# Seven block products on fp16 for the keys and values of the second attention layer

## The chip, the cores and the metric

The kernel runs on one core of a Trainium2 chip. The core has a matrix engine (TensorE; PE in the profile, with its weight loads as PEld), three elementwise engines (VectorE, DVE; ScalarE, ACT; GpSimd, POOL), and SyncE, whose queue (SP, SPq) issues the DMAs. Each engine works through its own list of instructions in the order written; semaphores make one wait for another. Matrix products accumulate in PSUM, eight banks of 128 x 512 fp32; all else lies in SBUF. The metric is the device time of one launch in microseconds (us), lower is better, as the median of several runs.

## The reference

Four layers in a row, A, B, A, B, with the same two sets of weights both times. The input has 2048 rows of 1024 in bf16.

```python
def _A_ref(x, wqkv, wo):                 # 32 heads of 32
    qkv = (x @ wqkv).reshape(B, S, 3, H, Dh).transpose(2, 0, 3, 1, 4)
    phi = lambda t: jnp.where(t > 0, t + 1, jnp.exp(t)) + 1e-6
    pq, pk = phi(q), phi(k)
    kv = jnp.einsum("bhsd,bhse->bhde", pk, v)
    z = jnp.einsum("bhsd->bhd", pk)
    num = jnp.einsum("bhqd,bhde->bhqe", pq, kv)
    den = jnp.einsum("bhqd,bhd->bhq", pq, z)[..., None] + 1e-6
    return (num / den).transpose(0, 2, 1, 3).reshape(B, S, D) @ wo
def _B_ref(x, w_gate, w_up, w_down):     # F = 3584
    return ((x @ w_gate) * (x @ w_up)) @ w_down
x = x + _A_ref(layernorm(x), wqkv, wo)   # then B, then A, then B
```

## The kernel before

**Layout.** X, the running 2048 x 1024 input, stays in SBUF as 16 tiles of 128 rows. Working memory is dealt out by hand from three queues (class `Free`): 16 `slots` of 128 x 4096 bf16, 13 `temps` of 128 x 512 fp32, and the 8 PSUM `banks`; the one returned first is handed out first. A write into one of them waits for its last reader. No scheduler orders anything: each engine's order is the order of the program, with small plans (`at(step, ...)`) that hang other work behind a numbered step of matrix products. A step is mostly 4 or 8 matmuls of 128 x 128 by 128 x 512.

**Layer A (`layer_A`, li = 0 and 2).** First the keys and values: `kv_chunk` makes one 128 x 512 piece of K or V of one row tile, 8 matmuls (L386); there are 64 chunks, each in a bank of its own. A key piece goes through `phi` (Exp on ACT, L210; min and add, L211, and max and add, L212, on DVE) into `pks`; a value piece is copied by ACT (L396) into `vbs`. `kp` (L405) multiplies keys with values into three banks `kvp` that are held through the stage; the rows of one group of 512 are multiplied while the next group is computed. Layernorm of the later row tiles runs in the same stage: `ln_stats` (L172, L175, DVE), `ln_norm` (L181, L183 on ACT, then L185 on DVE), and `tr_tile`, a transposing DMA on SP (L197). After that come the queries (`q_step`, L508), the denominators (L522), and the output products (L538). `rows`, `scan` and `load_rows` of the first layer A also measure the norms of the B weights, from which `scale_begin` and `scale_end` (L283 to L296) make power-of-two scales, so that B can run on fp16.

**Layer B (`ffn_pass`, twice per layer; q = 0 to 3 over the kernel).** A pass handles 1024 rows. Its up stage (`quad`, j = 0 to 13, L667) already uses a seven-product form of a 2 x 2 block product: of 14 products of 4 matmuls per quad, which write 6 of the 8 banks, ACT copies partial sums out (L672, L678, L722), DVE adds and multiplies (L683, L686) into `hs`. Seven slots of `hs` hold h, each the h of two quads. For q = 0 and 1 the weights are cast to fp16 by ACT, four casts per quad (L329), and four sums of them are made by DVE (L344). Its down stage (`down_seven`, L889) runs seven products of 14 steps each, in the order 1, 5, 6, 3, 7, 2, 4, with 98 steps of 4 matmuls. Each product reads two pieces of `w_down` (7 steps each); after each piece `load_piece` (L619 from a cache in DRAM, L623 from the input) asks for the one three pieces later, and ACT casts the pieces of products 1, 3 and 2 (L634, two halves) 7 steps ahead of use. `s_sum` (L811) makes the sums of h; `after` (L862) reads the four banks of a finished product on DVE. Into the same steps the plan puts the layernorm of the next stage's row tiles: `ln_stats` at 2 + 7u, `ln_norm` at 4 + 7u, the transpose at 5 + 7u, for eight tiles u in the first pass and four in the second; in the second pass of the first layer B also the loads of the K and V weights of the second layer A (`load_a` at steps 16, 30, 44, 75).

SP's list matters twice. A transpose waits there for its normalised tile, and a load waits for its slot; everything behind it in the list waits too.

Of the kernel before, what the change touches and what calls it, by code (L numbers as in the profile page):

```python
# [10 lines left out]
ALU = mybir.AluOpType  # L11
# [8 lines left out]
HS = 2.0 ** -35  # L20

# [13 lines left out]
def kernel(  # L35
# [45 lines left out]
    slots = Free([const.tile([P, 4096], BF16, tag=f"s{i}", name=f"s{i}") for i in range(16)])  # L81
    temps = Free([const.tile([P, NB], F32, tag=f"f{i}", name=f"f{i}") for i in range(13)])
# [47 lines left out]
    mask = const.tile([P, P], F32, tag="mask", name="mask")  # L130
# [18 lines left out]
    wst = const.tile([P, 32, 6], F32, tag="wst", name="wst")  # L149
    dsq = const.tile([P, 8], F32, tag="dsq", name="dsq")  # L150
    dmx = const.tile([P, 6], F32, tag="dmx", name="dmx")
    bexp = const.tile([P, 3], F32, tag="bexp", name="bexp")
    scw = const.tile([P, 3], F32, tag="scw", name="scw")
# [8 lines left out]

    xnTs = {}
    xqs = {}
    lns = {}
# [10 lines left out]

    def ln_norm(li, t):
# [6 lines left out]
        xn = xnp.tile([P, D], F16 if half else BF16, tag="xn", name="xn")  # L184
# [4 lines left out]
    def tr_tile(li, t):  # L189
# [5 lines left out]
        xnT = (h3 if li % 2 == 1 else v3)(s, NB)  # L195
# [11 lines left out]
    def phi(b, dst):  # L207
        m = temps.get()
        e = m[:].bitcast(BF16)[:, 0:NB]
        nc.scalar.activation(out=e, in_=b[:], func=ACT.Exp)  # L210
        nc.vector.tensor_scalar(out=e, in0=e, scalar1=1.0, scalar2=1e-6, op0=ALU.min, op1=ALU.add)  # L211
        nc.vector.scalar_tensor_tensor(out=dst, in0=b[:], scalar=0.0, in1=e, op0=ALU.max, op1=ALU.add)  # L212
        temps.put(m)
# [14 lines left out]

    def load_rows(r):
# [14 lines left out]
    qsum = {}  # L244

    def norm_sums(m, q):
        if m == 0:
# [3 lines left out]
            nc.vector.bn_aggr(out=mv[:], in_=wst[:])  # L251
# [3 lines left out]
                                           op0=ALU.mult, op1=ALU.add)  # L255
        else:
# [5 lines left out]
    def scale_begin(m):  # L262
        n = 2 - m
        q = small.tile([P, 2], F32, tag="wq2", name="wq2", bufs=1)
# [4 lines left out]
        qb = t[:].bitcast(BF16)[:, 0:2 * P].rearrange("p (m n) -> p m n", n=P)  # L269
# [5 lines left out]
    def scale_end(m):  # L275
        n = 2 - m
        q, t, qb = qsum.pop(m)
        b = banks.get()
        pt = b[:].bitcast(BF16)[:, 0:2 * P].rearrange("p (m n) -> p m n", n=P)
# [5 lines left out]
        e = bexp[:, 2 * m:2 * m + n]  # L285
# [5 lines left out]
        sc = scw[:, 2 * m:2 * m + n]  # L291
        nc.vector.reciprocal(out=sc, in_=e)
        nc.vector.tensor_scalar(out=sc, in0=sc, scalar1=WS, scalar2=None, op0=ALU.mult)
# [82 lines left out]
    def layer_A(li, ahead):  # L376
        pks = {}
        kvp = [banks.get() for _ in range(3)]
# [80 lines left out]

        kvx = slots.get()  # L460
# [88 lines left out]
        for i in range(NQ + OLAG):  # L549
# [4 lines left out]
            if i == 0:  # L554
                for t in range(NT - TPG, NT):
                    kp(t)
# [427 lines left out]
```

## Time and profile before

| what | us |
|---|---|
| three runs | 1510.39, 1510.46, 1511.22 (median 1510.46) |
| the profiled execution | 1511.85, of which the span on the core is 1509.8 |
| first layer A, to the first matmul of layer B | 251.56 |
| first layer B: up, down, up, down | 169.22, 84.61, 169.21, 84.61 |
| keys and values of the second layer A | 116.17 (759.21 to 875.38) |
| rest of the second layer A | 123.36 (875.38 to 998.74) |
| second layer B: up, down, up, down | 169.21, 84.61, 169.21, 84.62 |

The stage times are read from the timeline of TensorE and from the chain of work that ended last. The page names a group of instructions as line, engine, operation, output <- input by the program's names, shape, count, then busy time, mean duration in ns, and the engine's idle time just before with what ended it. A matmul's mean of 379 ns is its whole passage; matmuls overlap, and what counts is the distance between starts. The granted clock of TensorE is 1.00 in every stage.

### The profile page before, as it was taken

The page shows a single profiled execution, that of the slowest core. Times are in us where ns is not written, and L with a number is a line of the kernel's source. Part 1 is how long each engine was busy: PE and PEld are TensorE (multiplying, and loading weights), DVE is VectorE, ACT ScalarE, POOL GpSimd, SP SyncE. Part 2 cuts the span into 40 slices and gives each one's busy share as a digit, 9 for nine tenths or more (in the row PEclk, how much of TensorE's full clock was granted, in tenths as well). Part 3 has the DMA queues.
Part 4 walks back from the last instruction along what each step waited for, and adds up shares of the span by engine and source line. Part 5 has one row for each costly group of instructions (what it writes and reads, how often), then busy time and mean ns, then how long its engine had stood idle before and what let it go on. Part 6 is the DMA issues. An engine that isn't in the chain of part 4 may idle for free.

```text
span 1509.8 us, 18303 instructions
## 1 busy us (share of the span) xinstructions
PE 1500.2 (99%) x7122; PEld 689.6 (46%) x7170; DVE 940.1 (62%) x1596; ACT 737.0 (49%) x1115; POOL 90.3 (6%) x46
## 2 busy tenths in 40 slices
PE   9999999999999999999999999999999999999999
PEld 4454444444444444444445444444444444444444
DVE  6567989988686666667255466864444853444452
ACT  4678875767534577662133365533335223333420
POOL 0000004972000000000000000000000000000000
PEclk9999999999999999999999999999999999999999
DMA  8696246464348788749413300563333678333523
GB/s 244 165 305 206 84 91 193 147 208 143 130 126 252 240 263 254 259 174 256 151 29 84 84 1 5 149 237 140 140 115 126 170 252 348 112 140 140 195 74 129
DMA packets 213415, 247.61 MB, mean 164 GB/s; under 512 B 68432, under 2 KB 189264, under 8 KB 202576
## 3 DMA queue, kind: packets, MB, share of 16 engines
q1 hardware_dynamic: 213328, 246.44, 51.9%
q8 instruction: 56, 0.92, 0.3%
q14 instruction: 31, 0.25, 0.1%
HBM read 189.79 MB, written 40.89 MB: 153 GB/s over the span
## 4 chain that ended last, share of the span: by engine, by line
PE 98%; DVE 1%; DMA 1%; issue 0%; SPq 0%; DVEq 0%
PE b L667 45%; PE b L889 22%; PE b L386 14%; PE b L508 7%; PE b L538 7%; PE b L405 1%; PE b L522 1%; DMA s<-in_A_wqkv_dram 1%; PE b L490 0%; DVE st L172 0%; DVE X L540 0%; SPq L92 0%; DVE s L530 0%; DVE xn L185 0%; SPq L98 0%
## 5 line engine op out<-in xcount | busy, mean ns | idle before, releaser
L667 PE MATMUL b<-s,s 128*128 128x512 f16 x3136 | 677.5, 379 | 0.0
L667 PEld LDWEIGHTS <-s 128*128 128x128 f16 x3136 | 306.8, 98 | 370.0
L889 PE MATMUL b<-s,s 128*128 128x512 f16 x1568 | 339.1, 379 | 0.0
L683 DVE TENSOR_TENSOR f<-f,b 128x512 f32<-128x512 f32 x232 | 159.1, 687 | 226.9 <-ACT f L672 212.4
L672 ACT COPY f<-b 128x512 f32<-128x512 f32 x284 | 166.0, 584 | 224.8 <-PE b L667 224.8
L889 PEld LDWEIGHTS <-s 128*128 128x128 f16 x1568 | 153.4, 98 | 185.0
L386 PE MATMUL b<-s,s 128*128 128x512 bf16 x1000 | 221.5, 379 | 3.1 <-DMA s<-in_A_wqkv_dram 1.6
L386 PEld LDWEIGHTS <-s 128*128 128x128 bf16 x1024 | 99.7, 98 | 121.3 <-issue 2.2
L634 ACT ACTIVATE s<-s,scw 128x1792 f16<-128x1792 bf16 x48 | 83.1, 1785 | 90.8 <-DMA s<-in_B_w_down_dram 54.4
L210 ACT ACTIVATE f<-b 128x512 bf16<-128x512 f32 x128 | 75.6, 596 | 105.9 <-PE b L386 83.5
L329 ACT ACTIVATE s<-s,scw 128x1024 f16<-128x1024 bf16 x112 | 123.0, 1151 | 3.8 <-DMA s<-in_B_w_gate_dram 3.5
L678 ACT COPY b<-b 128x512 f32<-128x512 f32 x104 | 59.2, 570 | 128.3 <-PE b L667 128.3
L508 PE MATMUL b<-s,s 128*128 128x512 bf16 x504 | 119.5, 379 | 0.3
L538 PE MATMUL b<-s,s 128*128 128x512 bf16 x496 | 117.7, 379 | 1.1 <-DVE s L530 0.3
L592 POOL TENSOR_SCALAR s<-s,scw 128x1024 f16<-128x1024 bf16 x28 | 88.6, 3182 | 258.9 <-DVE X L540 245.0
L686 DVE SCALAR_TENSOR_TENSOR s<-f,b 128x512 f16<-128x512 f32 x108 | 74.2, 687 | 40.1 <-PE b L667 24.4
L211 DVE TENSOR_SCALAR f<-f 128x512 bf16<-128x512 bf16 x128 | 36.9, 288 | 81.0 <-ACT f L210 80.4
L686 DVE SCALAR_TENSOR_TENSOR s<-f,f 128x512 f16<-128x512 f32 x116 | 83.2, 718 | 4.0
L172 DVE BATCH_NORM_STATS2 st<-X 128x6 f32<-128x512 bf16 x128 | 81.9, 680 | 3.5 <-DMA X<-in_A_x_dram 3.5
L538 PEld LDWEIGHTS <-s 128*128 128x128 bf16 x512 | 50.0, 98 | 61.0 <-DVE s L530 1.0
L508 PEld LDWEIGHTS <-s 128*128 128x128 bf16 x512 | 50.0, 98 | 59.6
L862 DVE SCALAR_TENSOR_TENSOR X<-b,kap,f 128x512 bf16<-128x512 f32 x48 | 32.7, 743 | 60.6 <-PE b L889 60.6
(84 smaller groups left out, 859.1 us busy)
## 6 DMA issues: line engine op xcount, KB each, us to landing
s<-wc SPq DMA_DIRECT2D x56, 1024.0 KB, 6.6
s<-dc SPq DMA_DIRECT2D x32, 896.0 KB, 5.9
wc<-s SPq DMA_DIRECT2D x28, 1024.0 KB, 4.8
s<-in_B_w_down_dram SPq DMA_DIRECT2D x24, 896.0 KB, 5.2
s<-in_B_w_down_dram SPq DMA_DIRECT2D x14, 1024.0 KB, 7.4
s<-in_B_w_gate_dram SPq DMA_DIRECT2D x28, 512.0 KB, 5.7
s<-in_B_w_up_dram SPq DMA_DIRECT2D x28, 512.0 KB, 6.4
s<-in_A_wqkv_dram SPq DMA_DIRECT2D x11, 1024.0 KB, 9.7
```

What stands on the lines that cost most here:

```text
L172: nc.vector.bn_stats(out=st[:, c, :], in_=X[:, t, c * FMAX:(c + 1) * FMAX])
L329: nc.scalar.activation(out=h, in_=v, func=ACT.Copy, scale=scw[:, m:m + 1])
L386: nc.tensor.matmul(out=b[:], lhsT=xnT[:, k, tl * P:(tl + 1) * P], rhs=w[:, k, :], start=(k == 0), stop=(k == KD - 1))
L508: nc.tensor.matmul(out=b[:], lhsT=w[:, k, j * P:(j + 1) * P], rhs=xnT[:, k, :], start=(k == 0), stop=(k == KD - 1))
L538: nc.tensor.matmul(out=b[:], lhsT=v3(pqs[g], G)[:, c, tl * P:(tl + 1) * P], rhs=v3(M[n], NB)[:, c, :], start=(c == 0), stop=(c == KD - 1))
L592: nc.gpsimd.tensor_scalar(out=h3(s, D)[:, i, :], in0=v3(s, D)[:, i, :], scalar1=scw[:, 2:3], scalar2=None, op0=ALU.mult)
L634: nc.scalar.activation(out=v.bitcast(F16)[:, r * w:(r + 1) * w], in_=v[:, r * w:(r + 1) * w], func=ACT.Copy, scale=scw[:, 2:3])
L667: nc.tensor.matmul(out=o[m][:], lhsT=W.get(j, m, st[i - 1], k), rhs=mv[i - 1][:, k, :], start=start and k == 0, stop=stop and k == KH - 1, ...
L672: nc.scalar.copy(out=d[m][:], in_=o[m][:])
L683: nc.vector.tensor_tensor(out=d[m][:], in0=d[m][:], in1=o[m][:], op=ALU.add)
L686: nc.vector.scalar_tensor_tensor(out=hv[:, 2 * (j % 2) + r, g * G:(g + 1) * G], in0=x[:], scalar=HS, in1=y[:], op0=ALU.mult, op1=ALU.mult)
L889: nc.tensor.matmul(out=bank[(key, tl)][:], lhsT=lhs(i, j, tl), rhs=h3(wd[2 * pi + j // WPC], NB)[:, j % WPC, :], start=(j == 0 and i in (1 ...
```

## The change

In the second layer A (li = 2) keys and values are no longer made by `kv_chunk` but by a new `kv_seven`, the same seven-product scheme as in layer B. The code of `kv_chunk` stays, as `kv_eight`, for the first layer A. A unit u (0 to 7) handles four blocks: two row tiles and two more of the same 512-row group (`tiles(u)`), against two column halves of K and of V. It runs 14 products of 4 matmuls (names like `6k`: product 6 for the keys), in five banks, which with `kvp` are all eight. A bank takes several products one after the other, with copies by ACT in between.

For this the weights and the normalised rows of that layer are fp16. The norms of K, Q and V weights are measured in the first down stage (`scan_a`: six loads of 1 MB, twelve squares on ACT), the scales made around quads 0 and 1 of the second pass (`scale_begin(2)`, `scale_end(2)`). The second down stage gets 16 casts of K and V weights on ACT (`cast_a`), their sums (`w_sum`), the layernorm of eight row tiles instead of four, and the first group's row sums (`x_sum`) on DVE. The other eight row tiles are normalised inside `kv_seven`, where ACT applies the norm (`ln_apply`) instead of DVE, and where the query weights are loaded and cast as well. Query, denominator and `kvm` take the scales along as operands. The products of keys and values that are left for the first query step (`rest`) are those of the last unit: 2 tiles instead of 4.

`hs` is cut otherwise: one slot holds the h of quads 0 and 1, and from quad 2 on, four quads share two slots, one for each column half `a`; the slots of half 0 are free after the sums of product 7, not only in product 4. There are 17 slots and 12 temps, one of which holds the statistics `wst` until the first scales are made in the first layer A; the block mask is bf16.

```diff
-    slots = Free([const.tile([P, 4096], BF16, tag=f"s{i}", name=f"s{i}") for i in range(16)])
-    temps = Free([const.tile([P, NB], F32, tag=f"f{i}", name=f"f{i}") for i in range(13)])
+    slots = Free([const.tile([P, 4096], BF16, tag=f"s{i}", name=f"s{i}") for i in range(17)])
+    temps = Free([const.tile([P, NB], F32, tag=f"f{i}", name=f"f{i}") for i in range(12)])
...
-    mask = const.tile([P, P], F32, tag="mask", name="mask")
+    mask = const.tile([P, P], BF16, tag="mask", name="mask")
...
-    wst = const.tile([P, 32, 6], F32, tag="wst", name="wst")
+    wtmp = temps.get()
+    wst = wtmp[:][:, 0:192].rearrange("p (c s) -> p c s", s=6)
...
+    ACOL = (1, 0, 2)
...
+    def cast_a(m, n, i):
+        s = wA["kqv"[m]][n]
+        nc.scalar.activation(out=h3(s, NB)[:, 2 * i:2 * i + 2, :], in_=v3(s, NB)[:, 2 * i:2 * i + 2, :],
+                             func=ACT.Copy, scale=scw[:, 3 + m:4 + m])
...
+    def w_sum(which, i):
+        if which not in wS:
+            wS[which] = slots.get()
+            if "d" not in wS:
+                wS["d"] = slots.get()
+        a11, a12, a21, a22, c, d = w_blocks(which)
+        s1, s2 = c[:, 0:KH], c[:, KH:KD]
+        o, x, y, op = ((s1, a21, a22, ALU.add), (s2, s1, a11, ALU.subtract), (d, a11, a21, ALU.subtract),
+                       (a21, a12, s2, ALU.subtract))[i]
+        nc.vector.tensor_tensor(out=o, in0=x, in1=y, op=op)
...
+        t1, t2, t3, t4 = (t[:, j] for j in range(4))
+        o, x, y = ((t1, b12, b11), (t2, b22, t1), (t3, b22, b12), (t4, b21, t2))[i]
+        nc.vector.tensor_tensor(out=o, in0=x, in1=y, op=ALU.subtract)
...
+    def ln_rstd(li, t):
+        mv = lns[(li, t)]
+        rstd = small.tile([P, 1], F32, tag="rstd", name="rstd")
+        nc.scalar.activation(out=rstd[:], in_=mv[:, 1:2], func=ACT.Ln, bias=eps5[:], scale=1.0)
+        nc.scalar.activation(out=rstd[:], in_=rstd[:], func=ACT.Exp, scale=-0.5)
+        nmr = small.tile([P, 1], F32, tag="nmr", name="nmr")
+        nc.vector.tensor_scalar(out=nmr[:], in0=mv[:, 0:1], scalar1=rstd[:], scalar2=-1.0, op0=ALU.mult, op1=ALU.mult)
+        lns[(li, t)] = rstd, nmr
+
+    def ln_apply(li, t):
+        rstd, nmr = lns[(li, t)]
+        xn = xnp.tile([P, D], F16, tag="xn", name="xn")
+        nc.scalar.activation(out=xn[:], in_=X[:, t, :], func=ACT.Identity, bias=nmr[:], scale=rstd[:])
+        lns[(li, t)] = xn
...
+            nc.scalar.activation(out=e, in_=b[:], func=ACT.Exp, bias=lns2[:, c:c + 1], scale=kaps[:, c:c + 1])
+            nc.vector.tensor_scalar(out=e, in0=e, scalar1=scw[:, 3 + c:4 + c], scalar2=epss[:, c:c + 1],
+                                    op0=ALU.min, op1=ALU.add)
...
+    def scan_a(i, h, got={}):
+        if h < 0:
+            got[i] = load_cols(wqkv_v, ACOL[i // 2] * DC + i % 2)
+            return
+        s = got[i]
+        v = s[:, 2048 * h:2048 * h + 2048]
+        c = i % 2 * 2 + h
+        nc.scalar.activation(out=v, in_=v, func=ACT.Square, accum_out=asq[:, i // 2, c:c + 1])
+        if h == 1:
+            slots.put(s)
...
+        elif m == 2:
+            nc.vector.tensor_reduce(out=q[:, 0:3], in_=asq[:], axis=AX.X, op=ALU.add)
+            nc.vector.tensor_scalar(out=q[:, 0:2], in0=q[:, 0:2], scalar1=2.0 ** -27, scalar2=None, op0=ALU.max)
...
+        nc.vector.tensor_scalar(out=sc, in0=sc, scalar1=AS if m == 2 else WS, scalar2=None, op0=ALU.mult)
+        if m == 2:
+            nc.vector.tensor_scalar(out=kaps[:], in0=e, scalar1=1.0 / AS, scalar2=None, op0=ALU.mult)
+            nc.scalar.activation(out=lns2[:], in_=sc[:, 0:2], func=ACT.Ln)
+            nc.vector.tensor_scalar(out=epss[:, 0:2], in0=sc[:, 0:2], scalar1=1e-6, scalar2=None, op0=ALU.mult)
+            nc.vector.tensor_tensor(out=epss[:, 2:3], in0=epss[:, 0:1], in1=sc[:, 1:2], op=ALU.mult)
...
+    def kv_seven(kvp):
+        plan = {}
+
+        def at(step, f, *args):
+            plan.setdefault(step, []).append((f, args))
+
+        for t in range(2 * TPG, NT):
+            i = 4 + 9 * (t - 2 * TPG)
+            at(i, ln_stats, 2, t, (0,))
+            at(i + 1, ln_stats, 2, t, (1,))
+            at(i + 3, ln_rstd, 2, t)
+            at(i + 5, ln_apply, 2, t)
+            at(i + 6, tr_tile, 2, t)
+        for g, i in ((1, 15), (2, 46), (3, 76)):
+            for j in range(4):
+                at(i + 2 * j, x_sum, g, j)
+        at(20, load_w, "q", 0)
+        at(21, load_w, "q", 1)
+        for n in range(DC):
+            for i in range(4):
+                at(31 + 11 * n + 2 * i, cast_a, 1, n, i)
+        at(92, lambda: wA.update(o=[load_cols(wo_v, n) for n in range(DC)]))
+
...
+        SEQ = "1k 5k 1v 6k 2k 6v 7k 5v 7v 2v 4k 3k 4v 3v"
...
+            for j, step in enumerate(SEQ.split()):
+                i, w = int(step[0]), step[1]
+                key = "b" if i == 2 else ("c" if i in (3, 5) else "a") + w
+                if key not in bk:
+                    bk[key] = banks.get()
+                if i == 1 and w == "k":
+                    bk["b"] = banks.get()
+                b = bk[key]
+                rhs = w_rhs(w, i)
+                for k in range(KH):
+                    nc.tensor.matmul(out=b[:], lhsT=lhs[i][:, k, pr * P:(pr + 1) * P], rhs=rhs[:, k, :],
+                                     start=k == 0 and (i in (1, 5) or i == 2 and w == "v"), stop=k == KH - 1,
+                                     skip_group_check=True)
+                if i == 1:
+                    if w == "k":
+                        nc.scalar.copy(out=bk["b"][:], in_=b[:])
+                    else:
+                        copy("1v", b)
+                elif i == 6:
+                    copy("6" + w, b)
+                elif i == 7:
+                    copy("7" + w, b)
+                    if w == "k":
+                        add(tm["7k"][:], "7k", bk["ck"])
+                        phi(tm["7k"], pk(1, 1), 0)
+                    else:
+                        add(vb(1, 1), "7v", bk["cv"])
+                    temps.put(tm.pop("7" + w))
+                elif i == 3:
+                    if w == "k":
+                        add(tm["6k"][:], "6k", b)
+                        phi(tm["6k"], pk(1, 0), 0)
+                    else:
+                        add(vb(1, 0), "6v", b)
+                    temps.put(tm.pop("6" + w))
+                    banks.put(bk.pop(key))
+                elif i == 2:
+                    if w == "k":
+                        phi(b, pk(0, 0), 0)
+                    else:
+                        add(vb(0, 0), "1v", b)
+                        temps.put(tm.pop("1v"))
+                        banks.put(bk.pop("b"))
+                elif i == 4:
+                    if w == "k":
+                        phi(b, pk(0, 1), 0)
+                    else:
+                        nc.scalar.copy(out=vb(0, 1), in_=w4(b))
+                    banks.put(bk.pop(key))
+                for f, args in plan.get(u * 14 + j, ()):
+                    f(*args)
+
...
+        for u in range(2 * NG):
+            unit(u)
+            if u > 0:
+                for t in tiles(u - 1):
+                    kp(t, u == 1 and t == 0, False)
+            if u % 2 == 1:
+                slots.put(xgs.pop(u // 2))
...
+        rest = kv_eight(li, kvp) if li == 0 else kv_seven(kvp)
...
+                        nc.vector.scalar_tensor_tensor(out=kvm[:, 3 * b + j, :], in0=src[:, j, 0:P],
+                                                       scalar=kaps[:, 2:3], in1=mask[:], op0=ALU.mult, op1=ALU.mult)
...
-                for t in range(NT - TPG, NT):
-                    kp(t)
+                rest()
...
+    def hpos(a, j):
+        return (0, 2 * a + j) if j < 2 else (1 + 2 * ((j - 2) // 4) + a, (j - 2) % 4)
...
-            if j % 2 == 0:
+            if j == 0:
                 hs.append(slots.get())
-            hv = h3(hs[j // 2], 2 * G)
+            elif j % 4 == 2:
+                hs.extend([slots.get(), slots.get()])
...
+            if q == 1 and j == 0:
+                scale_begin(2)
+            if q == 1 and j == 1:
+                scale_end(2)
...
+            if i == 7 and r in (2, 4, 6):
+                slots.put(hs[r - 1])
...
-            for u in range(2 * TPG if p == 0 else TPG):
+            for u in range(2 * TPG):
                 t = nl[1] * 2 * TPG + u
-                at(2 + 7 * u, ln_stats, nl[0], t)
-                at(4 + 7 * u, ln_norm, nl[0], t)
-                at(5 + 7 * u, tr_tile, nl[0], t)
+                i = 2 + 7 * u if p == 0 or u < TPG else 56 + 9 * (u - TPG)
+                at(i, ln_stats, nl[0], t)
+                at(i + 2, ln_norm, nl[0], t)
+                at(i + 3, tr_tile, nl[0], t)
...
+                    for i in range(6):
+                        at(2 + 9 * i, scan_a, i, -1)
+                        at(10 + 9 * i, scan_a, i, 0)
+                        at(13 + 9 * i, scan_a, i, 1)
...
-                at(16, load_a, "k", 0)
-                at(30, load_a, "k", 1)
-                at(44, load_a, "v", 0)
-                at(75, load_a, "v", 1)
+                for i, (t0, t1, m) in enumerate(((10, 20, 0), (24, 34, 0), (38, 48, 2), (58, 68, 2))):
+                    at(t0, load_w, "kqv"[m], i % 2)
+                    for j in range(4):
+                        at(t1 + 2 * j, cast_a, m, i % 2, j)
+                for j in range(4):
+                    at(64 + 2 * j, w_sum, "k", j)
+                    at(79 + 2 * j, w_sum, "v", j)
+                    at(72 + 2 * j, x_sum, 0, j)
```

(`w_blocks`, `w_rhs` and `x_blocks`, left out, only name parts of the slots; `copy` and `add` inside a unit are an ACT copy from a bank to a temp and a DVE add of a temp and a bank.)

## Prediction

> **What bounds the kernel now.** I read first the page's busy times and the chain that ended last, then the stages one by one as windows, then the timelines of ACT and DVE at the places that the change touches.
>
> ```profile
> PE 1500.2 (99%) x7122; PEld 689.6 (46%) x7170; DVE 940.1 (62%) x1596; ACT 737.0 (49%) x1115; POOL 90.3 (6%) x46
> ...
> PE 98%; DVE 1%; DMA 1%; issue 0%; SPq 0%; DVEq 0%
> ...
> 251.73 169.22 PE b L667 x784
> ```
>
> TensorE is never without work, so time is the number of matmuls. 784 of them take 169.22 us, 0.2158 each; 4 (a step) take 0.863. The windows (busy time of PE, PEld, DVE, ACT, POOL; clock; DMA) show how much room the others have where the change puts work:
>
> ```profile
> 420.78:505.39 84.61, 84.61 (x393) 38.35 (x392) 60.42 (x100) 29.79 (x34) 0.00 (x0) 1.00 0.70 213
> ...
> 674.60:759.21 84.61, 84.61 (x394) 38.34 (x392) 43.72 (x72) 19.16 (x18) 0.00 (x0) 1.00 0.61 182
> 759.21:875.38 116.17, 115.54 (x598) 55.77 (x609) 56.37 (x116) 42.02 (x87) 0.00 (x0) 1.00 0.27 64
> ```
>
> First and second down stage, and the keys and values (KV): half-empty ACT and DVE. The prices come from these rows (groups, then timelines of ACT and DVE):
>
> ```profile
> L212 DVE SCALAR_TENSOR_TENSOR s<-b,f 128x512 bf16<-128x512 f32 x32 | 22.1, 692 | 1.1
> L210 ACT ACTIVATE f<-b 128x512 bf16<-128x512 f32 x32 | 19.1, 597 | 62.8 <-PE b L386 61.7 <-remote 1.1
> ...
> 506.45 0.58 ACT L672 COPY f<-b 128x512 f32<-128x512 f32 x1 [11.31 <-PE b L667]
> ...
> 514.71 3.23 ACT L329 ACTIVATE s<-s,scw 128x1024 f16<-128x1024 bf16 x3
> 518.60 0.57 ACT L678 COPY b<-b 128x512 f32<-128x512 f32 x1 [0.67 <-PE b L667]
> ...
> 521.40 0.68 DVE L344 TENSOR_TENSOR s<-s,s 128x1024 f16<-128x1024 f16 x1
> ...
> 178.87 0.42 DVE L283 TENSOR_REDUCE wq<-b 128x2 f32<-128x256 bf16 x1
> 179.32 0.17 DVE L287 TENSOR_SCALAR bexp<-wq 128x2 int32<-128x2 int32 x1
> ```
>
> A copy starts 0.2 after its product's last step (506.45 against 505.39 + 0.863). ACT starts back to back 0.1 early (copy or Exp 0.5, cast 1.07), DVE 0.08 early (0.61 per add, `bn_stats` or 128x1024 fp16 sum). ACT to DVE takes 0.04; I take 0.05 towards PE.
>
> **The change, part by part.**
>
> *Removed.* 64 chunks x 8 = 512 matmuls become 8 units x 14 x 4 = 448: -64 x 0.2158 = -13.8 us, all on the path. fp16 costs what bf16 costs (379 ns in both groups of the page). `kp` is the same 16 tiles.
>
> *The KV stage's two other queues.* A unit is 14 x 0.863 + 0.945 for two tiles of `kp` = 13.03 us. ACT has 7 copies and 4 Exps (5.5 us), DVE 5 adds and 4 phi pairs (about 7). Walked through in order, such a unit has no PE wait: the tightest copies (of 1, 6 and 6v, whose bank takes the next product two steps = 1.73 later) have 1.73 - 0.2 - 0.58 - 0.05 = 0.9 to spare. But extras stand in the same lists, in front of these copies: per layernorm tile 2 `bn_stats`, an aggregate (0.21) and a small product on DVE, 0.5 of rstd and 1.15 of `ln_apply` (by L329, same size) on ACT; in units 1, 3 and 5 four `x_sum` of 0.69 on DVE; in units 2 and 3 eight casts of 1.15 on ACT. One such extra eats the 0.9, two do not fit. And ACT stands still where an Exp waits for DVE's add (product 7 or 3), or rstd for DVE's aggregate. Five of eight banks in rotation, all in use, leave PE nothing else to do.
>
> I walked units 0 to 5 by these prices, PE, ACT and DVE lists side by side, time from the stage's start. The boundary of units 1 and 2 as an example: in unit 1 DVE has 24 instructions, 12.6 us, from 14.2 on; the last, the key add of product 3, ends at 28.0, and product 5 of unit 2, wanted at 27.33, overwrites its bank: 0.72. Behind that add ACT runs Exp to 28.64, rstd to 29.07, copy 4v to 29.55: 1v, wanted at 28.91, waits 0.69. Then `ln_apply` 29.9 to 31.05, and only then the copy of 1k to 31.5: 6k, wanted at 30.46, waits 1.11. Sums: entering unit 1 0.8, in it 0.5, entering unit 2 2.5, in it 0.8, entering unit 3 1.0, in it (four casts, a norm, three x_sums) 3.5, entering unit 4 2.6, in 5 0.5, in 0, 6 and 7 nothing. Together +12.2. Bounds: 0 (the stage before shows no such wait, though with a fresh bank per chunk; nothing here can gain beyond the matmuls), and 20 (some 80 ACT instructions in the loaded units without their 0.1 overlap: +8). I take the walk, since its rows are of the same instructions.
>
> *Scales at quads 0 and 1 of the second pass.* Three transposes: +0.2 (L281: two in 0.28). `scale_end(2)` ends in a Ln on ACT that waits for a DVE chain, and stands ahead of quad 1's first copies; product 6 of that quad waits for the first copy. DVE is busy with four weight sums until 522.0. Then the reduce (0.42 for 256 columns, 0.28 for 128: 0.56 for 384), five dependent small ones at 0.2, done at 523.6; Ln (0.29, by rstd's 294 ns) to 523.9; the copy, 518.60 before, to 524.5. Product 6 was due at 505.39 + 12.08 + 0.2 + 2.59 = 520.3. PE waits +4.2. Bounds 3.5 and 5: order and durations are all shown; only handovers are open. Behind the Ln stand no loads; DVE and ACT are level again in quad 1.
> [...] In this trace the granted clock is 1.00 throughout and no PE gap exceeds 1.5 us, so no row shows what a 4 us gap does. [...]
>
> *First down stage: `scan_a`.* Twelve squares of 128x2048 (L237: 1.90 + 0.19) are 25 us more on ACT, beside 30 of 84.6; six loads of 1 MB go into a DMA share of 0.70. ACT's list is in order: a square that waits for its load holds up rstd of the next tile, so DVE's xn, so that tile's transpose on SP, so the `w_down` piece behind it. Landings come from the second down stage:
>
> ```profile
> s<-in_A_wqkv_dram SPq DMA_DIRECT2D x1, 1024.0 KB, 9.7
> ...
> s<-in_B_w_down_dram SPq DMA_DIRECT2D x1, 896.0 KB, 9.8
> ```
>
> That is, 9.7 behind another piece, 9.8 for a piece behind such a load, against 5.5 alone. So scan 2, issued at 440.2 behind piece 5, lands at 449.9, its squares end at 453.8, transpose 4 goes from 451.7 to 454.9, piece 7 lands at 462, and its cast, also behind scan 3, has its first half at 463.6, wanted at 463.1: 0.5. Transpose 6 moves from 463.8 to 466.6, piece 9 stands behind scan 5 and lands at 476 to 478, wanted at 475.7. I take +1.5; bounds 0 (pieces land in 5.5) and 4 (each of pieces 7 and 9 at 9.8 behind a late transpose).
>
> *Second down stage.* ACT +16 casts (18 us on 19), DVE four tiles, eight `w_sum` (1.22 by L368), four `x_sum`: 66 of 84.6. Piece 6's cast stands behind one cast_a, piece 7's behind three; each still ends about 1 us before its use. DVE is behind from step 56 on but done by step 93 of 98; SP's four more transposes stand ahead of piece 11, which leaves at step 63 as it did before (729.6). POOL's list is unchanged. So 0; bounds 0 and 2 (both covers gone).
>
> *No cost taken.* 12 temps: a temp returns after some 7 us, DVE's lag is under 1. `hs`, `rest`, scaled phi, `kvm`, bf16 mask: same sizes and counts per stage; loads of weights still wait for slots freed 10 to 13 steps before the cast. Cover gone: under 1 us each.
>
> **Sum.** -13.8 + 12.2 + 0.2 + 4.2 + 1.5 = +4.3. Against the profiled execution (1511.85: span 1509.8 and 2.05 around it) 1516.2; that execution lies 1.4 above the median of the runs, 1510.46, so **1514.8** is forecast.
>
> **Rivals.** *The queues keep up (faster).* Place: the copies of products 1 and 6 in units 1 to 4. For it: by busy time ACT has some 24 us of work in 26 of units 2 and 3, which fits if waits do not add up. Price: no KV wait at all gives 1510.46 - 13.8 + 0.2 + 4.2 + 0 = 1501.1; with half of the walk's waits and the scan's 1.5, 1508.7. It decides when KV and scan waits together stay under 6.4. Against it: 0.9 of slack against casts of 1.07.
> *A wash.* These waits between 6.4 and 12.4: 1507.4 to 1513.5.
> *The first down stage becomes bound by its pieces.* Each late piece delays rstd, transposes and the next piece; SP's order speaks for it, and that TensorE's own delay gives it back against it. With 4 instead of 1.5, and 3 more in KV: 1520.
> *The stage does not shorten at all* would need slower fp16 matmuls: excluded by the 379 ns of both.
>
> **How the numbers follow.** A measurement tells 0.2% (3 us) from nothing. Chances: forecast and worse, 1513.5 to 1518, 0.42; over 1518, 0.16; the wash 0.24; under 1507.4 0.18. Slower 0.58, same 0.24, faster 0.18. Range: 1506 (5 of the 12 us of KV waits, none at the scans) to 1520, which leaves out about two in ten; the forecast's own range is 1511 to 1518.
>
> **What would show it.** In the new profile: 448 fp16 matmuls in a KV stage of about 115 us; PE waits there for ACT copies and DVE adds, most in units 1 to 3, none in the last two; one gap of 4 us three products into quad 1 of the second pass, released by ACT; waits under 2 us in the first down stage, released by ACT's cast or a DMA. Wrong if the KV stage is under 108 us (lists keep up), if the gap at quad 1 is missing, or if waits appear in stages that I priced at nothing, the second down stage above all.

## The result and the profile after

The changed kernel takes 1520.88 us (median of 6 runs, 1519.95 to 1521.35) against 1510.61 for the kernel before, run beside it: ratio 1.0066, 95% interval 1.0053 to 1.0079. It is slower, as forecast, but by 10.3 us instead of 4.3, and 0.9 us past the upper end of the range. The profiled execution took 1521.27 us, with a span of 1519.5; that of before had 1509.8, so 9.7 us have to be found.

The page of the changed kernel (busy times, then the chain that ended last, by engine):

```profile
PE 1495.6 (98%) x7109; PEld 683.2 (45%) x7109; DVE 987.5 (65%) x1675; ACT 814.7 (54%) x1196; POOL 89.6 (6%) x46
...
PE 92%; DVE 4%; ACT 3%; DMA 1%; issue 0%; SPq 0%; DVEq 0%
```

TensorE is busy for less time than before (1495.6 instead of 1500.2), and yet the span is longer: the chain now runs through DVE and ACT for 7% of it. The five largest waits of TensorE in the whole kernel say where (line waiting, releaser, us in total, times, longest):

```profile
PE b L539 <- ACT f L523: 5.1, 7, 1.4
PE b L539 <- DVE f L526: 4.6, 5, 1.3
PE b L909 <- ACT b L920: 4.0, 1, 4.0
PE b L539 <- ACT vb L576: 1.9, 5, 0.7
PE b L539 <- ACT b L544: 1.7, 2, 1.1
```

L539 is the product of the KV stage, L909 that of the up stages. The windows of the first down stage, the second, the KV stage, and the second up stage (PE, PEld, DVE, ACT, POOL; granted clock; DMA):

```profile
419.70:504.31 84.61, 84.61 (x394) 38.31 (x393) 60.15 (x100) 52.18 (x58) 0.00 (x0) 1.00 0.93 288
680.37:764.98 84.61, 84.61 (x394) 38.31 (x392) 62.70 (x100) 37.46 (x42) 0.00 (x0) 1.00 0.66 194
764.98:886.03 121.05, 107.23 (x561) 50.29 (x560) 79.45 (x149) 73.85 (x119) 0.00 (x0) 1.00 0.21 53
504.31:680.37 176.06, 172.10 (x788) 77.42 (x787) 111.57 (x179) 115.51 (x163) 0.00 (x0) 0.98 0.73 233
```

Both down stages are as long as before to the hundredth. The KV stage is 121.05. Its window holds 14 tiles of `kp`, where the window of before (116.17) holds 12, so like against like it is 121.05 against 117.1: +3.9. Without any wait it would be 448 x 0.2158 + 14 x 0.4725 = 103.3, so the waits cost 17.7. The waits listed for L539 add up to less, 13.8 with a small sixth one, because a profile counts an idle time from the modelled end of a matmul, 379 ns after its start, while the next could have started after 216: each of the twenty waits costs some 0.16 more than it shows, 3.3 together. The second up stage took 176.06 instead of 169.22: +6.84. Its one gap, on PE, ACT and DVE, in three timelines:

```profile
516.56 2.75 PE L909 MATMUL b<-s,s 128*128 128x512 f16 x12
523.27 2.29 PE L909 MATMUL b<-s,s 128*128 128x512 f16 x5 [3.96 <-ACT b L920]
```

```profile
522.53 0.20 ACT L381 ACTIVATE lns<-scw 128x2 f32<-128x2 f32 x1 [5.69 <-DVE scw L378]
522.64 1.06 ACT L920 COPY b<-b 128x512 f32<-128x512 f32 x2
```

```profile
520.32 0.69 DVE L434 TENSOR_TENSOR s<-s,s 128x1024 f16<-128x1024 f16 x1
520.92 0.55 DVE L368 TENSOR_REDUCE wq<-b 128x3 f32<-128x384 bf16 x1
521.51 0.17 DVE L372 TENSOR_SCALAR bexp<-wq 128x3 int32<-128x3 int32 x1
```

The copies of the quad stand behind the Ln, the Ln behind the chain of DVE, the chain behind four weight sums: 3.96 us, 4.2 forecast. From the gap on the window view (TensorE alone; the third number from the end is the granted clock) has

```profile
520.00:522.00 2.00, 0.00 (x0) 0.92 0.20 82
522.00:523.00 1.00, 0.00 (x0) 0.50 0.94 336
523.00:524.00 1.00, 0.73 (x2) 0.50 1.18 328
...
527.00:528.00 1.00, 1.00 (x4) 0.50 1.19 309
528.00:529.00 1.00, 1.00 (x5) 0.75 1.09 263
529.00:530.00 1.00, 1.00 (x7) 1.00 0.06 12
```

A finer cut of the same view puts the half clock between 521.7 and 528.5, 6.8 us. It begins inside the gap, 2.4 us after the last matmul ended (519.3), and lasts 5.2 us beyond it, which costs 2.6 us. (The view counts each matmul that touches a window, so the 4 of a half-clock microsecond stand against 6 or 7 at full clock.) The balance of the span, from these windows: -13.8 (64 matmuls) + 17.7 (KV waits) + 6.8 (gap, its clock and three transposes) - 1.1 (the first up stage began at 250.48 instead of 251.56; at the kernel's start TensorE waited 0.7 us for loads of weights instead of 1.6) = +9.6. The last term is no effect of the change: in the fifteen other profiles below, with the same code up to there, the second up stage begins anywhere from 503.88 to 505.52 (504.31 here, 505.39 before).

### The profile page after: what moved, and what is told of

The parts are those of the page before. It is cut to its first block, busy times and chain, and to the rows that moved or that the text cites. A ratio compares the mean times of both kernels' runs of the same rounds, so it can differ in the third digit from the quotient of the medians.

```text
span 1519.5 us, 18411 instructions
## 1 busy us (share of the span) xinstructions
PE 1495.6 (98%) x7109; PEld 683.2 (45%) x7109; DVE 987.5 (65%) x1675; ACT 814.7 (54%) x1196; POOL 89.6 (6%) x46
## 4 chain that ended last, share of the span: by engine, by line
PE 92%; DVE 4%; ACT 3%; DMA 1%; issue 0%; SPq 0%; DVEq 0%
PE b L909 44%; PE b L1146 22%; PE b L746 7%; PE b L609 7%; PE b L777 7%; PE b L539 2%; ACT f L277 1%; PE b L760 1%; DVE st L220 1%; DVE s L280 1%; ACT xn L237 1%; DMA s<-in_A_wqkv_dram 1%; PE b L628 0%; DVE f L526 0%; PE b L727 0%; DVE f L278 0%
## 5 line engine op out<-in xcount | busy, mean ns | idle before, releaser
L909 PE MATMUL b<-s,s 128*128 128x512 f16 x3136 | 680.4, 380 | 4.0 <-ACT b L920 4.0
L909 PEld LDWEIGHTS <-s 128*128 128x128 f16 x3136 | 307.1, 98 | 376.2 <-issue 7.6
L1146 PE MATMUL b<-s,s 128*128 128x512 f16 x1568 | 339.1, 379 | 0.0
L1146 PEld LDWEIGHTS <-s 128*128 128x128 f16 x1568 | 153.3, 98 | 185.2
L746 PE MATMUL b<-s,s 128*128 128x512 bf16 (+1 forms) x512 | 120.3, 379 | 0.0
L777 PE MATMUL b<-s,s 128*128 128x512 bf16 x512 | 118.5, 379 | 0.3 <-DVE s L769 0.3
L875 ACT ACTIVATE s<-s,scw 128x1792 f16<-128x1792 bf16 x48 | 83.0, 1783 | 61.6 <-DMA s<-in_B_w_down_dram 54.2
L539 PE MATMUL b<-s,s 128*128 128x512 f16 x448 | 101.6, 379 | 13.8 <-ACT f L523 5.1
L609 PE MATMUL b<-s,s 128*128 128x512 bf16 x512 | 112.1, 379 | 0.9 <-DMA s<-in_A_wqkv_dram 0.7
L777 PEld LDWEIGHTS <-s 128*128 128x128 bf16 x512 | 50.0, 98 | 60.9 <-DVE s L769 1.0
L609 PEld LDWEIGHTS <-s 128*128 128x128 bf16 x512 | 49.6, 98 | 60.6 <-issue 1.2
L746 PEld LDWEIGHTS <-s 128*128 128x128 bf16 (+1 forms) x512 | 49.9, 98 | 59.4
L539 PEld LDWEIGHTS <-s 128*128 128x128 f16 x448 | 43.4, 97 | 69.3 <-issue 20.6
L1057 DVE TENSOR_TENSOR s<-s,s 128x1024 f16<-128x1024 f16 x80 | 52.9, 678 | 23.3 <-PE b L1146 23.3
```

The costliest lines, as they stand in the source:

```text
L539: nc.tensor.matmul(out=b[:], lhsT=lhs[i][:, k, pr * P:(pr + 1) * P], rhs=rhs[:, k, :], start=k == 0 and (i in (1, 5) or i == 2 and w == "v ...
L609: nc.tensor.matmul(out=b[:], lhsT=xnT[:, k, tl * P:(tl + 1) * P], rhs=w[:, k, :], start=(k == 0), stop=(k == KD - 1))
L746: nc.tensor.matmul(out=b[:], lhsT=w[:, k, j * P:(j + 1) * P], rhs=xnT[:, k, :], start=(k == 0), stop=(k == KD - 1))
L777: nc.tensor.matmul(out=b[:], lhsT=v3(pqs[g], G)[:, c, tl * P:(tl + 1) * P], rhs=v3(M[n], NB)[:, c, :], start=(c == 0), stop=(c == KD - 1))
L909: nc.tensor.matmul(out=o[m][:], lhsT=W.get(j, m, st[i - 1], k), rhs=mv[i - 1][:, k, :], start=start and k == 0, stop=stop and k == KH - 1, ...
L1146: nc.tensor.matmul(out=bank[(key, tl)][:], lhsT=lhs(i, j, tl), rhs=h3(wd[2 * pi + j // WPC], NB)[:, j % WPC, :], start=(j == 0 and i in (1 ...
```

## Experiments

All of them start from the changed kernel. The stage lengths are of one profile each; where an edit did not touch the KV stage, five profiles (the changed kernel's among them) gave 121.03 to 121.08. They run from the stage's first product to the first product of the queries.

### What the KV stage costs without its extras

The stage was run without its extras (the layernorm, the first five lines; the block differences; the casts of the query weights), and without each kind. The buffers are still handed out, so the later stages read what happens to stand in them.

```
-            at(i, ln_stats, 2, t, (0,))
-            at(i + 1, ln_stats, 2, t, (1,))
-            at(i + 3, ln_rstd, 2, t)
-            at(i + 5, ln_apply, 2, t)
-            at(i + 6, tr_tile, 2, t)
...
-                at(i + 2 * j, x_sum, g, j)
...
-                at(31 + 11 * n + 2 * i, cast_a, 1, n, i)
```

> Leaves out, in the keys-and-values stage, the layernorm of its eight row tiles, the block differences of row groups 1 to 3 and the eight casts of the query weights (later stages read what happens to stand in those buffers). ACT then has only 7 copies and 4 Exps per unit, DVE 5 adds and 4 phi pairs. Theory: the stage is longer than its matmuls because copies and adds stand behind those extras; without them it takes 448 x 0.2158 + 14 x 0.4725 = 103.3 us, at most 105, against 121.06 with them, and the whole about 1504. Rival: the rotation over five banks alone, with an Exp of 0.8 us behind each add, is what makes TensorE wait; then 112 us or more stay.

Measured: 1503.62 us (ratio 0.995, 0.9927 to 0.9972). The stage, in the window view:

```profile
765.11:868.55 103.44, 103.44 (x561) 50.46 (x560) 59.85 (x105) 55.56 (x87) 0.00 (x0) 1.00 0.10 31
```

No wait at all, and 103.44 us, as the count of matmuls has it. So five rotating banks with copies and adds behind them keep up by themselves; the whole 17.6 us come with the extras in the queues. Each kind alone:

> Leaves out only the eight casts of the query weights in the keys-and-values stage (units 2 and 3; the query stage multiplies weights that were not scaled). If the eight casts are the main cause, the stage falls from 121.1 by the waits of units 2, 3 and of the way into 4, some 6 us, to 115. If each extra only fills slack that the next extra needs too, less than 4 us go.

> Leaves out only the layernorm of the eight row tiles in the keys-and-values stage (statistics, rstd, normalization, transposes; the units read what stands in the buffers). Two tiles fall into each of units 0 to 4 and they are the only extra in unit 0, the end of 2 and 4: by the walk of the prediction about 8 of its 12.2 us, so of the measured 17.7 some 11 us: 110. If casts and block differences decide, 117 or more.

> Leaves out only the twelve block differences of row groups 1 to 3 in the keys-and-values stage (units 2 to 7 multiply what stands in those buffers). They are 0.69 us each on DVE, in units 1, 3 and 5. If DVE lists of single units decide, the stage falls by about 4 us to 117; if ACT alone decides, by under 1.

| left out | time, one run | KV stage | saved |
|---|---|---|---|
| casts | 1517.67 | 117.53 | 3.5 |
| layernorm | 1507.34 | 107.40 | 13.7 |
| block differences | 1517.96 | 117.71 | 3.3 |
| all three | 1503.62 | 103.44 | 17.6 |

The casts met their second expectation (under 4 us: they fill slack that others need too), the block differences their first, and the layernorm saved more than the 11 us expected (of its eight tiles two fall into each of units 0, 2 and 4, one into 1 and 3). It costs most, and the three savings sum to 20.5, more than 17.6: they share slack. TensorE's waits without the layernorm were 0.9, 0.8 and 0.8 us in all, with the casts and differences still in place.

### Whether the walk or its prices were wrong

The prediction priced the stage's Exp at 0.60 us and DVE's first half of phi at 0.29, by the first layer's form. The profile of the changed kernel has the pointer form:

```profile
L277 ACT ACTIVATE f<-f,lns,kaps 128x512 bf16<-128x512 f32 x16 | 13.0, 813 | 28.3 <-DVE f L526 28.3
L277 ACT ACTIVATE f<-b,lns,kaps 128x512 bf16<-128x512 f32 x16 | 12.4, 775 | 3.8 <-PE b L539 3.8
...
L278 DVE TENSOR_SCALAR f<-f,scw,epss 128x512 bf16<-128x512 bf16 x31 | 12.7, 410 | 36.0 <-ACT f L277 36.0
```

```
-            nc.scalar.activation(out=e, in_=b[:], func=ACT.Exp, bias=lns2[:, c:c + 1], scale=kaps[:, c:c + 1])
-            nc.vector.tensor_scalar(out=e, in0=e, scalar1=scw[:, 3 + c:4 + c], scalar2=epss[:, c:c + 1],
-                                    op0=ALU.min, op1=ALU.add)
+                nc.scalar.activation(out=e, in_=b[:], func=ACT.Exp, scale=2.0 ** -24)
+                nc.vector.tensor_scalar(out=e, in0=e, scalar1=1.0, scalar2=1e-6, op0=ALU.min, op1=ALU.add)
```

Only the calls in `kv_seven` take this form.

> In the keys-and-values stage the Exp takes a constant scale and no bias, and DVE's first half of phi takes constants, instead of a pointer to one number per partition each; the features that come out are therefore not the reference's. The prediction priced these at 0.60 and 0.29 us, by the first layer's form, where the pointer forms measured 0.80 and 0.41. If that pricing is why the waits came to 17.7 us instead of 12.2, the stage falls by about 5 us to 116, and the Exp takes 0.60. If the walk missed for another reason (handovers, the order), by less than 2.

Measured (one run): 1515.25 us, the KV stage 115.82. The groups:

```profile
L278 ACT ACTIVATE f<-f 128x512 bf16<-128x512 f32 x16 | 10.1, 629 | 26.4 <-DVE f L530 26.4
L278 ACT ACTIVATE f<-b 128x512 bf16<-128x512 f32 x16 | 9.5, 594 | 4.6 <-PE b L543 4.6
L279 DVE TENSOR_SCALAR f<-f 128x512 bf16<-128x512 bf16 x32 | 9.3, 291 | 33.1 <-ACT f L278 33.1
```

With the prices that the walk assumed for phi, the waits are 115.82 - 103.44 = 12.4 us; the walk gave 12.2. The total could agree by luck, so here are the units one by one. Each number is the time from one pair of `kp` tiles to the next (the first from the stage's start), less the same stretch of the bare stage:

| waits, us, in unit | 0 and 1 | 2 | 3 | 4 | 5 | 6 | 7 |
|---|---|---|---|---|---|---|---|
| the walk | 1.3 | 3.3 | 4.5 | 2.6 | 0.5 | 0 | 0 |
| with constants | 1.34 | 3.30 | 4.58 | 2.60 | 0.34 | 0.22 | 0.00 |
| the changed kernel | 2.87 | 4.27 | 5.68 | 2.91 | 0.95 | 0.92 | 0.01 |

The walk was right, and two prices, 0.2 and 0.12 us too low, 32 times each, made 5.2 us of waits; which of the two did more was not separated. The prices act only together with the extras: the bare stage has the dear Exp too, and no wait.

The profile of the kernel before could have told the price of the Exp. Its denominators have a Ln of the same size with one pointer (`eps`) and an Exp without:

```profile
L524 ACT ACTIVATE f<-b,eps 128x512 f32<-128x512 f32 x64 | 44.1, 689 | 35.0 <-PE b L522 35.0
L527 ACT ACTIVATE f<-f 128x512 bf16<-128x512 f32 x64 | 40.3, 630 | 2.0
```

The Ln takes 689 ns where the Exp from PSUM without a pointer (L210) takes 597, 92 more. It is not the function: `rstd` of 128x1, a Ln with a pointer, takes 294 and its Exp without one 203, while the Ln of the scales, which has no pointer, took 0.20 us above. Two pointers at 92 ns make 0.78 from PSUM and 0.81 from SBUF, an estimate from these rows, and 775 and 813 were measured.

### The gap in the second pass, and the clock

First the Ln was taken out of `scale_end` and so out of the way of the copies:

```
-            nc.scalar.activation(out=lns2[:], in_=sc[:, 0:2], func=ACT.Ln)
...
+            if q == 1 and j == 2:
+                nc.scalar.activation(out=lns2[:], in_=scw[:, 3:5], func=ACT.Ln)
```

> The Ln of the scales is issued two quads later instead of ahead of quad 1's copies. Theory: the gap of 4.0 us goes, and with it the 6.83 us at half clock behind it (2.6 us), so 1520.9 - 4.0 - 2.6 = 1514.3, and the granted clock is 1.00 throughout. Rival 1: the clock's loss is not tied to the gap: 1516.9. Rival 2: the gap comes back at the next product, because the copies still wait for the four weight sums of DVE: over 1518.

Measured: 1514.6 us (9 runs; ratio 1.0025, 1.0015 to 1.0035). No wait of TensorE is left in the stage, which takes 169.38 us (505.52 to 674.90) against 169.22 before, and the granted clock is 1.000 in every run. Against the changed kernel that is -6.3 (1520.88 to 1514.6, with the kernel before at 1510.61 and 1510.83 beside them), gap and clock together, as the theory said; rivals 1 and 2 fall.

Then the chain was moved on DVE only, in front of the four weight sums, behind the second, or behind the third (the call then stands between two sums of `W.sums(2)`), to make gaps of other sizes:

```
-            if q == 1 and j == 1:
-                scale_end(2)
...
             quad(j)
+            if q == 1 and j == 0:
+                scale_end(2)
             W.release(j)
```

> The scale chain stays ahead of quad 1's copies, but DVE does it before the four weight sums of that quad instead of behind them. Theory: the Ln is done 4 x 0.69 = 2.8 us earlier and the gap shrinks from 4.0 to about 1.3 us; a gap of that size leaves the clock at 1.00, so 1520.9 - 2.7 - 2.6 = 1515.6. Rival 1: a short gap costs the clock as well: 1518.2. Rival 2: the sums, now behind, hold up the quad's sixth product: the gap moves there and the time stays within 2 us of 1520.9.

> The scale chain stands between the second and the third weight sum of DVE instead of behind the fourth: a gap of TensorE of about 2.7 us (1.4 with no sum ahead, 4.0 with four). [...]

> The chain behind the third of four sums: a gap of about 3.35 us. [...]

| sums ahead of the chain | gap, us | second up stage in the profile | time, us | mean clock of the runs |
|---|---|---|---|---|
| 0 | 1.43 | 170.97 | 1516.83 (ratio 1.0037, 1.0024 to 1.0049) | 1.000 in all of 6 |
| 2 | 2.75 | 172.29, at full clock | 1518.88 (1.005, 1.0031 to 1.007) | 1.000, 1.000, 0.999, 0.999 |
| 3 | 3.35 | 174.58 | 1520.15 (1.006, 1.0037 to 1.0083) | 0.999 in all of 3 |
| 4, the changed kernel | 3.96 | 176.06 | 1520.88 | 0.999 three times, 0.997 three times |

Against the 169.38 without a gap, the first two stages are longer by the gap and 0.16 (the modelled end of a matmul, as in the KV stage). The third has 1.7 more, half of the 3.4 us at half clock that its profile shows behind the gap, and the fourth 2.6 more, half of the 5.2 us that lie behind the gap there. With no sum ahead the time came out 1.2 us above the expected 1515.6, but at full clock.

With three sums ahead, TensorE's timeline and then its windows:

```profile
522.65 7.67 PE L911 MATMUL b<-s,s 128*128 128x512 f16 x27 [3.35 <-ACT b L922]
```

```profile
522.00:523.00 1.00, 0.35 (x2) 0.94 0.00 0
523.00:524.00 1.00, 1.00 (x4) 0.50 0.38 139
...
526.00:527.00 1.00, 1.00 (x6) 0.85 1.19 229
527.00:528.00 1.00, 1.00 (x6) 1.00 0.64 184
```

By the shares of the window view the half clock lasts 3.4 us here, from 522.9, 0.2 us after the matmuls resumed, to 526.3. With the gap of 3.96 us it lasts 6.8 us in the changed kernel's profile, from 2.4 us after the last matmul on, and 3.4 us, all behind the gap, in the profiles with constants in phi, without the casts and without the layernorm. All sixteen runs of kernels that kept this gap have a mean clock of 0.997 to 0.999. With two sums ahead, a gap of 2.75 us, it depends on the run: 1518.15 and 1518.64 at 1.000, 1519.12 and 1519.49 at 0.999. What decides whether and when the half clock sets in was not shown.

### Easing the queues

If the extras cause the waits, taking them off the busy queue, or uncoupling ACT and DVE, should recover time with nothing left out. Normalization on DVE (which also makes the small product `nmr` unnecessary), and casts on POOL:

```
-        nc.scalar.activation(out=xn[:], in_=X[:, t, :], func=ACT.Identity, bias=nmr[:], scale=rstd[:])
...
+        nc.vector.tensor_scalar(out=xn[:], in0=X[:, t, :], scalar1=mv[:, 0:1], scalar2=rstd[:],
+                                op0=ALU.subtract, op1=ALU.mult)
...
-                at(31 + 11 * n + 2 * i, cast_a, 1, n, i)
+                at(31 + 11 * n + 2 * i, cast_p, 1, n, i)
...
+    def cast_p(m, n, i):
+        s = wA["kqv"[m]][n]
+        for k in (2 * i, 2 * i + 1):
+            nc.gpsimd.tensor_scalar(out=h3(s, NB)[:, k, :], in0=v3(s, NB)[:, k, :],
+                                    scalar1=scw[:, 3 + m:4 + m], scalar2=None, op0=ALU.mult)
```

> In the keys-and-values stage DVE normalizes the eight row tiles (as it does elsewhere) instead of ACT: ACT loses 8 x 1.24 = 9.9 us of work, DVE gains about 8 x 0.4. If the 1.24 us instruction on ACT is what the copies stand behind, half of the 13.7 us that leaving the whole layernorm out saved, some 7, go: stage 114 us. Rival: the waits come from the coupling (rstd on ACT waiting for DVE's aggregate, 5.6 us of ACT idle time), which stays: under 3 us go.

> The eight casts of the query weights run on POOL, which has nothing to do in this stage, instead of ACT (some 25 us of POOL work beside it). Theory: the stage falls by what leaving them out saved, 3.5 us, to 117.5. Rival: POOL slows DVE, and the stage stays at 120 or more.

The first measured 1514.81 us with a stage of 115.1 (-5.9, a little less than half of the layernorm's share), the second 1519.72 with 119.15 (-1.9, little more than half of what leaving the casts out gave). POOL needs 1.6 us per 512 columns, 24.9 in all, and DVE's `tensor_scalar` of phi went from 410 to 452 ns beside it; that this is the rest of the difference was not shown. Together with the late Ln, and then with rstd one product later and the differences spaced:

> Three edits together: the Ln two quads later, the eight row tiles normalized on DVE, the query casts on POOL. If the theory of lists holds, 1514.6 (the Ln alone) - 7 - 3.5 = about 1504, under the kernel before. If the parts overlap, 1508; if the coupling of rstd is the cause, 1511 or more.

> As the three edits together, and rstd and the normalization one product later after the statistics, the block differences one in three products instead of one in two. If ACT's idle time before rstd (5.6 us, four times) makes waits on the chain, 2 us less than without these two edits; if not, within 0.7 us of it.

1508.26 (0.9985, 0.9976 to 0.9994) and 1506.89 (0.9976, 0.9967 to 0.9986), stages of 114.7 and 113.4: below the kernel before, but 10 us of waits were left. The savings overlapped, as in the middle case of the first expectation, and the spacing gave 1.4, between the two cases of the second. TensorE waited most for adds of DVE:

```profile
PE b L543 <- DVE f L530: 2.8, 3, 1.3
PE b L543 <- DVE vb L530: 2.5, 2, 1.8
```

The first row is the key add of product 3, at the boundaries of units, with 1.9 us of waits for ACT behind it; the second is the value add of product 7, in front of the last product of a unit. DVE's list at the boundary is: add of 2v, phi of 4k (waits for its Exp), add of 3k, phi of 3k (waits again). So DVE's half of each phi was put behind the next product's add (`phi_open` issues the Exp and keeps DVE's two instructions in a list, `flush` issues them):

```
-                        phi(b, pk(0, 1), 0)
+                        phi_open(b, pk(0, 1), partial(banks.put, bk.pop(key)))
...
                         add(tm["6k"][:], "6k", b)
-                        phi(tm["6k"], pk(1, 0), 0)
+                        flush()
+                        phi_open(tm["6k"], pk(1, 0), partial(temps.put, tm.pop("6k")))
```

> In the keys-and-values stage DVE's half of each phi is issued one product later, so that the add of product 3 no longer stands behind DVE's wait for the Exp of product 4 (DVE idles 36 us on such waits in this stage). Nothing else is changed. If that coupling of ACT and DVE makes the waits at the unit boundaries (0.9 to 1.3 us each, released by the key add, and the 0.3 to 0.7 us behind them), some 5 us go: stage 116. If the extras in the lists are enough by themselves, under 2 us go.

> The three edits (Ln two quads later, row tiles normalized on DVE, query casts on POOL), DVE's half of phi one product later, and the layernorm steps and block differences put at the products of a unit where DVE has least. If the couplings are what is left of the waits, the stage falls from 113.4 us to 107 or less and the whole to 1500; if the lists are simply full, it stays within 1 us of 1506.9.

Alone, one run: 1511.24 us, the stage 112.2, so -8.8 instead of the 5 expected. The waits of TensorE for DVE's key adds fell from 4.6 us to

```profile
PE b L562 <- DVE f L549: 0.3, 1, 0.3
```

while those for the copies into temps only went from 5.1 to 4.3. With everything together, and the steps of the layernorm, the differences and the casts placed one by one, 1498.68 us (4 runs; ratio 0.9919, 0.9902 to 0.9935): 12 us faster than the kernel before. That is the first case of the expectation, in which the couplings were what was left. The window of its KV stage, and the only wait left in it:

```profile
759.45:863.97 104.52, 103.61 (x562) 50.45 (x561) 83.68 (x151) 58.71 (x104) 26.32 (x16) 1.00 0.25 61
```

```profile
PE b L565 <- DVE vb L552: 0.9, 1, 0.9
```

DVE does more here (83.7 us) than in the changed kernel (79.5), ACT less by 15, POOL 26, and TensorE waits for them once, 0.9 us. Of the 13.8 us that the change takes away, 12 are there to be had; which queue the other work is in, and in what order, decides whether they are. How the gain divides between place and order was not separated here; the order of phi alone gave 8.8 in the stage.

## Why the prediction was right and wrong

- *Direction*: right, and not by luck: the KV waits and the gap together outweigh the 13.8 us, in the forecast as in the measurement.
- *64 matmuls fewer, -13.8*: right. The bare stage is 103.44 long, for 103.3 by count.
- *KV waits, +12.2*: right in mechanism and place (waits at the units named, released by copies and adds, in the last two units only two of 0.3), mis-sized by 5.5. The failed step is the price list: "copy or Exp 0.5" back to back, by the first layer's Exp, which has neither a pointer scale nor a bias. The changed one takes 0.775 to 0.813, DVE's part 0.41 instead of 0.29. With the assumed forms the waits are 12.4, and they fall on the units as walked. The walk's bound of 20 held the measured 17.7, but the upper end of the range, 1520, took in only 3 us more in this stage.
- *Scale gap, +4.2*: right, 3.96, in the place forecast and released by ACT.
- *The clock behind the gap, nothing in the sum*: wrong. No row of before shows a gap of 4 us, and the sum has only its length. Every run of the changed kernel has a mean clock of 0.997 or 0.999, and the profiled execution 6.8 us at half clock. The stage is 6.68 longer than without the gap (176.06 against 169.38), and less the gap (4.1 with the modelled end of the matmul) that is 2.6 for the clock.
- *First down stage, +1.5*: wrong, 0. The chain ran as described, but shorter. ACT stood still 8.9 us in three waits for loads of the scan:

```profile
447.31 1.91 ACT L304 ACTIVATE s<-s 128x2048 bf16<-128x2048 bf16 x1 [3.99 <-DMA s<-in_A_wqkv_dram]
...
459.10 3.45 ACT L875 ACTIVATE s<-s,scw 128x1792 f16<-128x1792 bf16 x2
```

  The step that failed is the landing of a scan behind a piece, put at 9.7: scan 2 took 8.0. So transpose 4 left 1.6 us later in the stage than before, not 3.2, and piece 7, which landed 5.2 us after its issue, was cast (L875, first half) some 1.1 us ahead of its use instead of 0.5 late. Piece 9 landed 0.8 us ahead of its own use. The DMA share was 0.93, and no product waited. The rival that made this stage the bound came out near the time measured, by luck: for a cause that was not there.
- *Second down stage and the rest, 0*: right, 84.61 both times.
- *Sum*: 5.5 (prices) + 2.4 (clock and gap together) - 1.5 (scans) - 1.1 (start of the kernel, scatter) = 5.3, which added to the forecast of 4.3 gives 9.6; the span grew by 9.7. The median lies 0.4 below the profiled execution, where the forecast took the 1.4 of before, and so misses by 6.1.
- *Queues keep up* (rival): not as the change was written, but they do in the last kernel, with work moved and reordered; "0.9 of slack against casts of 1.07" was no reason against it in principle. By their busy times alone ACT (73.9 us) and DVE (79.5) had room in a stage of 103; their lists did not use it.

## What to carry to other kernels

When a change shortens the engine that is the bound, price the other queues by the very form of instruction that the new code issues: a pointer scale and bias made this Exp three tenths longer, and where two lists wait on each other such an error grows into waits. A row of the same engine with the same kind of operand, in the profile at hand, may already have the price. Where ACT and DVE hand work to and fro (add, Exp, phi), put something independent between a request and its answer: moving DVE's half of phi by one product took 8.8 us off the stage, more than moving the normalization to DVE (5.9) or the casts to POOL (1.9). And look at the clock behind a gap of TensorE: here one of 3.35 us cost 1.7 us more than its length and one of 3.96 us 2.6 more. The mean clock was under 1 in every run with these gaps, and with one of 2.75 in two of four.

## What the runs showed of the hardware that was not expected

- Exp on 128x512 with pointer scale and bias: 775 ns from PSUM, 813 from SBUF, against 594 and 629 with a constant scale and no bias. DVE's `tensor_scalar` min-and-add on bf16: 410 ns with pointers, 291 with constants.
- The same normalization of 128x1024 (bf16 to fp16) took 1239 ns on ACT and 542 on DVE.
- Mean granted clock of a run with a gap of TensorE in the second pass: 1.000 with 1.43 us (all six runs); 1.000 twice and 0.999 twice with 2.75 us; 0.999 with 3.35 us (three of three); 0.997 to 0.999 with 3.96 us (all sixteen runs that kept it). Behind the 3.35 us the profile has 3.4 us at half clock, which cost 1.7 us (174.58 less 169.38 and a gap of 3.35 + 0.16).
